# A planned transformer block: a look-ahead on VectorE, the first K and V groups apart, and a new ScalarE cost

## The chip, the cores and the metric

The kernel runs on one core of one Trainium2 chip. The metric is the device time of one launch in microseconds (us). Five engines run in parallel, each through its own queue in order: TensorE (PE, matmuls, with its weight loads shown as PEld), ScalarE (ACT), VectorE (DVE), GpSimd (POOL) and SyncE (SP, which issues the DMAs). They meet through semaphores. A matmul writes PSUM, whose banks hold 512 fp32 values per partition; ACT or DVE then copies or combines the result into SBUF, which is called an evacuation here. Until it is done, the bank can't take another group of matmuls.

## The reference

One block: layer norm, multi-query attention with 32 heads and one shared K and V, a residual, layer norm, a gated feed-forward part, a residual. S = 2048 tokens, D = 1024, head width 32, F = 3584, all in bf16.

```python
q = (x @ wq).reshape(B, S, H, Dh)          # x is the normed input
k = x @ wk                                 # one K and V for all heads
v = x @ wv
scores = einsum("bhqd,bkd->bhqk", q, k) * Dh ** -0.5
o = einsum("bhqk,bkd->bhqd", softmax(scores), v)
h = x0 + o.reshape(B, S, D) @ wo           # x0 is the raw input
g, u = ln(h) @ w_gate, ln(h) @ w_up
out = h + (sigmoid(g) * u) @ w_down
```

## The kernel before

**A plan, then the streams.** The Python program does not emit instructions at once. It first runs a planner (class `Plan`) that keeps its own clock in ns for each engine, and it decides from that clock what each engine does next. Only the resulting order, one list per engine, is then emitted, with semaphore waits between engines. The chip keeps the order; its times are its own. So a changed cost in the plan changes no instruction, only the order of instructions.

- PE is planned by a loop (from line 952). At each step it looks at the plan's PE clock `t`. If the backlog of ACT is under 750 ns and the next scores are possible, it emits a *score visit* (`emit_S`); else it goes on with the current matmul group, or picks a new one from the queues in the order `PRIO`: xT, KV, Q0, OP, GU, D, Q. A group needs a bank of `F_ps` that is free by the plan's clock.
- ACT, DVE, POOL and SP have a heap each. `Plan.step` takes the engine that can start first, at time `s`, and on it the ready operation with the lowest `prio` number (line 89). An operation is ready at `o.ready`, when all that it depends on has ended by the plan. Costs come from `t_act`, `t_dve` and `t_mm`: `occ` is how long the engine is taken, `lat` when the result can be used.

**Priorities on DVE.** 0: the evacuations of attention outputs (L688, L692, L697, L701, L709) and of the up projection (L895). 1: those of the output projection (L777), of Q and K, and the scaling in the first norm (L369). 2: others, also the down projection's (L925). 3: norm statistics and the merge of row sums (L654). 4: the row-sum adds (L647).

**Attention.** Queries are taken in 16 tiles of 128 tokens; each tile has 4 pairs of head groups `G`, and a pair needs 8 visits over the keys. A visit is 8 matmuls (K = 32 rows, four packed in the rows of the array) into `S_ps` (6 banks), and two exponentials (L613) of 128x1024 that ACT writes to probability slots `Pr`. For the softmax sums DVE adds the probability tiles into `Ts` (L647), one add per exponential, merges the halves (L654), and PE multiplies the merged tile by ones. The products with V run in two halves of 8 key tiles, `mk_PV(G, 0)` and `mk_PV(G, 1)`, each 32 matmuls packed in the columns. The first half leaves its bank by one copy to `Oc` (L692); the second by an add to `Oc` (L697) and a transpose of the sums (L709), after which reciprocal, transpose and product follow. A slot comes free once its PV group and its add are done; without two free slots no score visit is possible.

**The rest on PE.** KV, Q, output projection (OP), gate and up (GU) and down (D) are groups of full-size matmuls. All these groups and PV share `F_ps`, which has two banks. GU weights come through a ring of 256 KB pieces by DMA. A gate group leaves its bank by a tanh on ACT (L891), an up group by L895 on DVE. All matmuls are emitted by the helper at L382, so the profile tells them apart by their tiles: `S_ps<-QTb,kT` scores, `F_ps<-Pr,Vb` and `F_ps<-Ts,ones` PV, `F_ps<-ring,hnT` GU, `F_ps<-zone,hact` D, `F_ps<-wo_sb,OT` OP, `F_ps<-zone` KV and Q.

**The start.** `mk_KV(p)` makes K for 256 tokens (8 matmuls with the replicated weight `wk4`) and V for the same tokens (16 small matmuls with `wv_sb`) as one group in one bank. It may be picked when the transposed input, the replicas of wk (4 copies on ACT, L313) and wv are there. K is evacuated to `kT4` (`k_ev`), V to `Vb` (`v_ev`). The first score visit needs K of the first pair and two Q groups, not V. `free_wd` loads pieces of w_down into room that the Q, K and V inputs leave.

Of the kernel before, what the change touches and what calls it, by code (L numbers as in the profile page):

```python
# [14 lines left out]
DH = 32  # L15
LN_EPS_BF16 = 1.0013580322265625e-05
SEM = 75.0


class Op:  # L20
# [16 lines left out]
class Plan:  # L37
# [39 lines left out]
    def step(self, limit):  # L77
        best = None
        for e in self.ENG:
            h = self.heap[e]  # L80
            if h:
                s = max(self.free[e], min(o.ready for o in h))
                if best is None or s < best[0]:
                    best = (s, e)
        if best is None or (limit is not None and best[0] > limit):
            return False
        s, e = best
        h = self.heap[e]
        o = min((o for o in h if o.ready <= s + 1e-9), key=lambda o: (o.prio, o.seq))
        h.remove(o)  # L90
        self.free[e] = s + o.occ
        if o.nbytes:
            go = max(s + 1400.0, self.dma_free["sp"])
            self.dma_free["sp"] = go + o.nbytes / 280.0
            o.end = self.dma_free["sp"] + 900.0
        else:
            o.end = s + o.lat
        o.pos = len(self.lists[e])
        self.lists[e].append(o)
        for u in o.users:  # L100
            u.ready = max(u.ready, o.end)
            u.missing -= 1
            if u.missing == 0:
                self.heap[u.eng].append(u)
        o.users = []
        return True
# [8 lines left out]


def t_act(n):
    return dict(occ=n / 1.2 + 60.0, lat=n / 1.2 + 170.0 + SEM)


def t_dve(n, rate=0.96, fix=158.0):
# [7 lines left out]
def bass_sequential_preLN__grouped_kv_mqa__glu_gated_glu__prompt_kernel(  # L129
# [15 lines left out]
    DT = D // P  # L145
    NT = S // P
# [13 lines left out]
    NPS = 16  # L160
    NX = 4
    NCR = 12
    NB = 3
    NPC = 22
    NST = 3
# [7 lines left out]
    with ExitStack() as es:  # L173
# [12 lines left out]
        kT4 = SB("kT4", [S])  # L186
        Vb = SB("Vb", [NT, DH])
# [22 lines left out]
        F_ps = EC(nc.psum_tensor("F_ps", [P, 2, 512], F32))  # L210
# [92 lines left out]
        wv_ld = dma(lambda: ACT.dma_start(wv_sb, A_wv.rearrange("(a p) j -> p a j", p=P)), "wv", P * DT * DH * 6, [x_ld[1]], prio=0, ring="act")  # L303
# [7 lines left out]
        rep_ops = []  # L311
# [124 lines left out]

        def queue_after_xT(t):
            if t % 2 == 1:
                queues["KV"].append(mk_KV(t // 2))
            if t == 1:  # L440
                for g in range(NG):
                    queues["Q0"].append(mk_Q(g, 0, 256))
            if 1 < t < 8 and t % 2 == 1:
                for g in range(NG):
                    queues["Q"].append(mk_Q(g, (t - 1) * P, 256))
            if t % 4 == 3 and t > 8:
                for g in range(NG):
                    queues["Q"].append(mk_Q(g, (t // 4) * 512, 512))
# [5 lines left out]
        wd_ld = []  # L454
        q_done = collections.Counter()

        def mk_KV(p):
            def atoms(b):
                r = []
                for dt in range(DT):  # L460
                    r.append((mm(F_ps[:, b, 0:256], wk4[:, dt, :], xnT(dt, p * 256, 256), dt == 0, dt == DT - 1),
                              256, rep_ops if dt == 0 else []))
                for k in range(2):
                    for dt in range(DT):
                        r.append((mm(F_ps[:, b, 256 + k * DH:256 + (k + 1) * DH],
                                     xnT(dt, p * 256 + k * P, P), wv_sb[:, dt, :],
                                     dt == 0, dt == DT - 1), DH, [wv_ld] if dt == 0 else []))
                return r

            def after(b, last):  # L470
                fa, fd = both(kT4[:, p * 256:(p + 1) * 256], F_ps[:, b, 0:256])
                k_ev[p] = evac(fa, fd, 256, [last], 1)
                fa, fd = both(Vb[:, 2 * p:2 * p + 2, :],
                              F_ps[:, b, 256:256 + 2 * DH].rearrange("p (a b) -> p a b", a=2))
                v_ev[p] = evac(fa, fd, 64, [last, k_ev[p]], 2)
                free_wd(last)
                return [k_ev[p], v_ev[p]]
            return Group("KV", atoms, lambda: [xT_ev[2 * p], xT_ev[2 * p + 1], rep_ops[-1], wv_ld], after)

        q_ready = collections.defaultdict(dict)  # L480
        q_store = []
# [51 lines left out]

        def free_wd(last):
            for i in list(wd_left):
                if (i < 4 and q_left4[i] == 0 and 2 * i in k_ev and 2 * i + 1 in k_ev) or \
                        (i in (4, 5) and all(q_done[g] == S for g in range(4 * i - 16, 4 * i - 12))) or \
                        (i == 6 and len(k_ev) == NT // 2):
                    wd_left.remove(i)
                    load_wd(4 * i, 4, [last])  # L540

# [404 lines left out]
        v = 0  # L946
        idle = 0

        def known(deps, t):
            return all(d is not None and d.end is not None and d.end <= t for d in deps)  # L950

        while True:
            t = pl.free["pe"]
            pl.advance(t)
            pump(t)
            if v < NV:
                run = max(pl.free["act"], t) + sum(o.occ for o in pl.heap["act"])
                sd = s_ready(v)
                can_s = sd is not None and known(sd, t)
                if can_s and run - t < 750.0:  # L960
                    emit_S(v)
                    v += 1
                    emit_PV(t)
                    idle = 0
                    continue
            else:
                sd, can_s = None, False
            if sd is None and queues["PV"]:
                if emit_PV(t):
                    idle = 0  # L970
                    continue
            if cur is not None:
                fn, n, deps, *cb = cur[1][cur_i]
                if known(deps, t) or not can_s:
                    o = emit_mm(fn, n, deps + (cur[2] if cur_i == 0 else []))
                    o.tag = cur[0].cls
                    if cb and cb[0]:
                        cb[0](o)
                    cur_i += 1
                    if cur_i == len(cur[1]):  # L980
                        bank_rel[cur_b] = cur[0].after(cur_b, o)
# [146 lines left out]
```

The softmax here doesn't subtract the row's maximum and nothing guards it: scores larger than these inputs give would overflow.

## Time and profile before

| what | value |
|---|---|
| time, median of 3 runs | 1103.32 us (1102.48 to 1103.97) |
| span of the profiled run | 1100.7 us |
| exponentials L613 on ACT, 128x1024 | 1024 (1014 into `Pr`, 10 into `wo_sb`), mean length 1078 ns |
| row-sum adds L647 on DVE, 128x1024 bf16 | 864, mean 680 ns for the most frequent form |
| up evacuation L895 on DVE, 128x512 | 112, mean 681 ns |
| `Oc` copy L692, add L697, transpose L709 (most frequent forms) | 60 each, 422, 419 and 441 ns |
| first exponential starts at | 19.76 us |

How to read it: lengths of single instructions overlap on an engine, so the step from one start to the next is shorter than the length. "Idle before" in a line of the profile is time in which the engine did nothing, with the instruction that ended it behind the arrow. Busy time of PE counts modelled ends of matmuls that are pipelined; a PE that reads 98% is not a PE at 98% of its peak.

### The profile page before, as it was taken

The numbers are of one execution on the slowest core, as the hardware profiler recorded it, in microseconds if no ns is written. First come the engines' busy times: TensorE is split into PE (matmuls) and PEld (weight loads), VectorE is DVE, ScalarE is ACT, GpSimd is POOL, SyncE is SP. The second block draws the span as 40 slices with busy tenths as digits, with TensorE's granted clock in tenths as the row PEclk, the third lists the DMA queues.
The fourth block names the chain that finished last, engine by engine and source line by source line (L and its number), as shares of the span: only waits on it lengthen the run. The fifth ranks groups of instructions, "written<-read, shape, count | busy, mean of one in ns | idle before, by whom it ended". The sixth has DMA issues, their size and how long they took to land.

```text
span 1100.7 us, 30884 instructions
## 1 busy us (share of the span) xinstructions
PE 1076.2 (98%) x12635; PEld 473.0 (43%) x12635; DVE 901.1 (82%) x1753; ACT 1009.7 (92%) x1164; POOL 31.1 (3%) x56
## 2 busy tenths in 40 slices
PE   8999999999999999999999999999999999999998
PEld 5663433444344444443444444443444444344443
DVE  8679988898888889898888979897888979898611
ACT  4999999999999999999999999999999999999310
POOL 1100000000000000000000000000000000000000
PEclk9999999999999999999999999999999999999999
DMA  9897499959678595978768594977869595977993
GB/s 260 180 287 231 128 261 243 278 134 277 163 181 233 147 253 131 251 188 214 228 167 237 152 250 127 250 203 199 232 153 245 144 249 149 245 197 170 264 272 118
DMA packets 310988, 228.13 MB, mean 207 GB/s; under 512 B 121920, under 2 KB 302144, under 8 KB 310848
## 3 DMA queue, kind: packets, MB, share of 16 engines
q1 hardware_dynamic: 308768, 226.04, 78.0%
q8 instruction: 99, 1.62, 0.6%
q10 hardware_dynamic: 2080, 0.13, 0.1%
q14 instruction: 41, 0.34, 0.1%
HBM read 195.69 MB, written 7.86 MB: 185 GB/s over the span
## 4 chain that ended last, share of the span: by engine, by line
PE 54%; ACT 24%; DVE 12%; issue 6%; DMA 4%; ACTq 0%; SPq 0%; DVEq 0%
PE F_ps L382 46%; ACT Pr L613 23%; PE S_ps L382 8%; DVE Ts L647 7%; DMA ring<-in_B_w_gate_dram 2%; DMA zone<-in_A_wv_dram 1%; ACT tnh L891 1%; DVE Rc L709 1%; DVE hst L895 1%; DVE Oc L697 1%; DVE h_sb L777 1%; DVE st L321 0%; DVE st L323 0%; DMA ring<-in_B_w_up_dram 0%; DMA zone<-ring 0%
## 5 line engine op out<-in xcount | busy, mean ns | idle before, releaser
L613 ACT ACTIVATE Pr<-S_ps 128x1024 bf16<-128x1024 f32 x1014 | 952.3, 1078 | 6.6 <-PE S_ps L382 6.6
L647 DVE TENSOR_TENSOR Ts<-Ts,Pr 128x1024 bf16<-128x1024 bf16 x732 | 484.2, 680 | 48.2 <-ACT Pr L613 45.2
L382 PE MATMUL F_ps<-ring,hnT 128*128 128x512 bf16 (+1 forms) x1889 | 443.8, 381 | 12.3 <-issue 3.7
L382 PEld LDWEIGHTS F_ps<-ring,hnT 128*128 128x128 bf16 (+1 forms) x1889 | 150.0, 98 | 220.0 <-issue 71.6
L382 PE MATMUL F_ps<-zone,hact 128*32 128x512 bf16 (+1 forms) x1196 | 221.8, 380 | 0.0
L382 PE MATMUL S_ps<-QTb,kT 32*128 32x256 bf16 x4096 | 203.3, 273 | 2.1 <-ACT Pr L613 1.7
L382 PEld LDWEIGHTS S_ps<-QTb,kT 32*128 32x128 bf16 x4096 | 60.6, 92 | 200.4 <-ACT Pr L613 140.6
L382 PE MATMUL F_ps<-Pr,Vb 128*32 128x256 bf16 x4056 | 134.5, 274 | 0.0
L382 PEld LDWEIGHTS F_ps<-zone,hact 128*32 128x32 bf16 (+1 forms) x1196 | 80.0, 97 | 95.9 <-issue 20.6
L891 ACT ACTIVATE tnh<-F_ps 128x512 f32<-128x512 f32 x112 | 73.3, 655 | 52.1 <-PE F_ps L382 52.0
L895 DVE SCALAR_TENSOR_TENSOR hst<-tnh,F_ps 128x512 bf16<-128x512 f32 x112 | 76.3, 681 | 46.0 <-PE F_ps L382 45.9
L382 PEld LDWEIGHTS F_ps<-Pr,Vb 128*32 128x32 bf16 x4056 | 96.9, 96 | 37.4 <-ACT tnh L891 16.1
L647 DVE TENSOR_TENSOR Ts<-Pr 128x1024 bf16<-128x1024 bf16 x126 | 84.7, 683 | 34.0 <-ACT Pr L613 33.9
L382 PE MATMUL F_ps<-zone 128*128 128x256 bf16 (+3 forms) x609 | 75.4, 281 | 5.1 <-DMA zone<-in_A_wv_dram 2.0
L382 PE MATMUL F_ps<-wo_sb,OT 128*128 128x512 bf16 (+1 forms) x271 | 63.7, 381 | 0.1
L382 PEld LDWEIGHTS F_ps<-zone 128*128 128x128 bf16 (+1 forms) x609 | 44.2, 97 | 27.4 <-issue 9.8
L925 DVE SCALAR_TENSOR_TENSOR h_sb<-F_ps,h_sb 128x512 bf16<-128x512 f32 x32 | 22.0, 688 | 40.6 <-PE F_ps L382 40.6
L654 DVE TENSOR_TENSOR Ts<-Ts 128x1024 bf16<-128x1024 bf16 x64 | 44.0, 688 | 1.4
L335 POOL TENSOR_SCALAR zb<-mvb 128x1 bf16<-128x1 bf16 (+1 forms) x24 | 10.9, 455 | 1008.1 <-DVE mvb L331 1008.1
L382 PEld LDWEIGHTS F_ps<-wo_sb,OT 128*128 128x128 bf16 (+1 forms) x271 | 21.4, 97 | 29.5 <-issue 6.8
L714 DVE STREAM_TRANSPOSE Rc<-Ri 128x256 f32<-128x256 f32 x64 | 28.2, 441 | 0.0
L697 DVE TENSOR_TENSOR Oc<-F_ps,Oc 128x256 f32<-128x256 f32 x60 | 25.2, 419 | 2.6 <-PE F_ps L382 2.5
(60 smaller groups left out, 338.4 us busy)
## 6 DMA issues: line engine op xcount, KB each, us to landing
ring<-in_B_w_gate_dram SPq DMA_DIRECT2D x320, 256.0 KB, 4.2
ring<-in_B_w_up_dram SPq DMA_DIRECT2D x320, 256.0 KB, 3.9
zone<-in_B_w_down_dram SPq DMA_DIRECT2D x28, 256.0 KB, 3.9
h_sb<-in_A_x_dram SPq DMA_DIRECT2D x16, 256.0 KB, 5.1
out_dram<-h_sb SPq DMA_DIRECT2D x32, 128.0 KB, 2.9
ring<-in_A_x_dram SPq DMA_DIRECT2D x7, 512.0 KB, 6.4
QTb<-q_scratch SPq DMA_DIRECT2D x14, 256.0 KB, 3.6
q_scratch<-hact SPq DMA_DIRECT2D x16, 128.0 KB, 3.2
```

The costliest lines, as they stand in the source:

```text
L335: f = pl.op("pool", lambda: POOL.tensor_scalar(out=zb[:, ph, sl].unsqueeze(2), in0=mvb[:, ph, sl, 1:2], scalar1=LN_EPS_BF16, scalar2=None, ...
L382: fn = lambda: PE.matmul(o, lhsT=l, rhs=r, start=start, stop=stop, **kw)
L613: exps[u] = pl.op("act", lambda slot=slot, pb=pb: ACT.activation(out=pslot(slot).rearrange("p (a b) -> p a b", a=2), in_=S_ps[:, pb:pb + 2 ...
L647: o = pl.op("dve", lambda T=T, a=a, b=b: DVE.tensor_tensor(out=T, in0=a, in1=b, op=ALU.add), deps, prio=4, **t_dve(1024, 1.92))
L654: merge_ev[G] = pl.op("dve", lambda T4=T4: DVE.tensor_tensor(out=T4[:, :, 0, :], in0=T4[:, :, 0, :], in1=T4[:, :, 1, :], op=ALU.add), [sum ...
L697: a = pl.op("dve", lambda: DVE.tensor_tensor(out=Oc[:, :], in0=O, in1=Ob, op=ALU.add), [last, oc_ev[G], o_ev.get(G - 1)], prio=0, **t_dve( ...
L709: c = pl.op("dve", lambda: DVE.transpose(out=Rc[:, :], in_=R), [last, o_ev.get(G - 1)], prio=0, **t_dve(256))
L714: d = pl.op("dve", lambda: DVE.transpose(out=Rc[:, :], in_=Ri[:, :].unsqueeze(2).to_broadcast([P, 2 * P // DH, DH])), [r], prio=2, **t_dve ...
L777: h_ev[(t, dc)] = pl.op("dve", lambda: DVE.tensor_tensor(out=h_sb[:, t % 4, sl], in0=F_ps[:, b, :], in1=h_sb[:, t % 4, sl], op=ALU.add), [ ...
L891: tanh_of[n] = pl.op("act", lambda: ACT.activation(out=tnh[:, n % 2, :], in_=F_ps[:, b, :], func=ACTF.Tanh, scale=0.5), [last, tn_user.get ...
L895: e = pl.op("dve", lambda: DVE.scalar_tensor_tensor(out=hst[:, n % NST, :], in0=tnh[:, n % 2, :], scalar=1.0, in1=F_ps[:, b, :], op0=ALU.a ...
L925: e = pl.op("dve", lambda: DVE.scalar_tensor_tensor(out=h_sb[:, t % 4, sl], in0=F_ps[:, b, :], scalar=0.5, in1=h_sb[:, t % 4, sl], op0=ALU ...
```

## The change

Three parts, and a fourth that is set to do nothing:

1. In `Plan.step`, if DVE is about to start an operation of priority 3 or more (a row-sum add, a merge, norm statistics), and an operation of priority 0 or 1 will be ready within `AHEAD` = 200 ns, DVE takes that one and waits for it. The purpose is that an evacuation that frees a PSUM bank does not stand behind an add that has just begun.
2. `t_act` gives each ScalarE operation a fixed part of 53 ns instead of 60 in `occ`. Exponentials, tanh and ACT copies are all planned by it. The purpose is to bring the plan's pace to the chip's.
3. For the first 256 tokens K and V are two groups, so that K no longer waits for wv. The frees of `free_wd` ask for V in place of K.
4. `pv_fits` can put off a PV group after a score visit; with `RM` = 0 its first condition always holds.

```diff
+AHEAD = 200.0
+PMAX = 1
...
         o = min((o for o in h if o.ready <= s + 1e-9), key=lambda o: (o.prio, o.seq))
+        if e == "dve" and o.prio >= 3:
+            soon = [x for x in h if x.prio <= PMAX and s < x.ready <= s + AHEAD]
+            if soon:
+                o = min(soon, key=lambda x: x.ready)
+                s = o.ready
         h.remove(o)
...
 def t_act(n):
-    return dict(occ=n / 1.2 + 60.0, lat=n / 1.2 + 170.0 + SEM)
+    return dict(occ=n / 1.2 + 53.0, lat=n / 1.2 + 170.0 + SEM)
...
+    RM = 0
+    PU = 3
...
             if t % 2 == 1:
-                queues["KV"].append(mk_KV(t // 2))
+                for part in (("k", "v") if t == 1 else ("kv",)):
+                    queues["KV"].append(mk_KV(t // 2, part))
...
-            return Group("KV", atoms, lambda: [xT_ev[2 * p], xT_ev[2 * p + 1], rep_ops[-1], wv_ld], after)
+            def first():
+                return [xT_ev[2 * p], xT_ev[2 * p + 1]] + ([rep_ops[-1]] if "k" in part else []) + ([wv_ld] if "v" in part else [])
+            return Group("KV", atoms, first, after)
...
-                if (i < 4 and q_left4[i] == 0 and 2 * i in k_ev and 2 * i + 1 in k_ev) or \
+                if (i < 4 and q_left4[i] == 0 and 2 * i in v_ev and 2 * i + 1 in v_ev) or \
...
+        def pv_fits():
+            left = 8 if cur is None else len(cur[1]) - cur_i
+            return left >= RM or len(queues["PV"]) > 1 or len(p_free) < PU or v >= NV
...
                     emit_S(v)
                     v += 1
-                    emit_PV(t)
+                    if pv_fits():
+                        emit_PV(t)
```

More of the change, by code (lines that the diff above doesn't have):

```diff
@@ L455, in bass_sequential_preLN__grouped_kv_mqa__glu_gated_glu__prompt_kernel, with mk_KV @@
         q_done = collections.Counter()
-        def mk_KV(p):
+        def mk_KV(p, part):
             def atoms(b):
                 r = []
-                for dt in range(DT):
+                for dt in range(DT if "k" in part else 0):
                     r.append((mm(F_ps[:, b, 0:256], wk4[:, dt, :], xnT(dt, p * 256, 256), dt == 0, dt == DT - 1),
                               256, rep_ops if dt == 0 else []))
-                for k in range(2):
+                for k in range(2 if "v" in part else 0):
                     for dt in range(DT):
@@ L470, in after @@
             def after(b, last):
[L471 to L477, printed above, removed]
-            return Group("KV", atoms, lambda: [xT_ev[2 * p], xT_ev[2 * p + 1], rep_ops[-1], wv_ld], after)
+                rel = []
+                if "k" in part:
+                    fa, fd = both(kT4[:, p * 256:(p + 1) * 256], F_ps[:, b, 0:256])
+                    k_ev[p] = evac(fa, fd, 256, [last], 1)
+                    rel.append(k_ev[p])
+                if "v" in part:
+                    fa, fd = both(Vb[:, 2 * p:2 * p + 2, :],
+                                  F_ps[:, b, 256:256 + 2 * DH].rearrange("p (a b) -> p a b", a=2))
+                    v_ev[p] = evac(fa, fd, 64, [last, k_ev[p]], 2)
+                    rel.append(v_ev[p])
+                    free_wd(last)
+                return rel
+            def first():
+                return [xT_ev[2 * p], xT_ev[2 * p + 1]] + ([rep_ops[-1]] if "k" in part else []) + ([wv_ld] if "v" in part else [])
+            return Group("KV", atoms, first, after)
         q_ready = collections.defaultdict(dict)
@@ L535, in free_wd @@
             for i in list(wd_left):
-                if (i < 4 and q_left4[i] == 0 and 2 * i in k_ev and 2 * i + 1 in k_ev) or \
+                if (i < 4 and q_left4[i] == 0 and 2 * i in v_ev and 2 * i + 1 in v_ev) or \
                         (i in (4, 5) and all(q_done[g] == S for g in range(4 * i - 16, 4 * i - 12))) or \
-                        (i == 6 and len(k_ev) == NT // 2):
+                        (i == 6 and len(v_ev) == NT // 2):
                     wd_left.remove(i)
```

## The prediction

> **What bounds the kernel now.** I read the page first (busy shares, then the 40 slices), then the windows by stage, then the waits, and last the timeline around single waits.
>
> ```profile
> PE 1076.2 (98%) x12635; PEld 473.0 (43%) x12635; DVE 901.1 (82%) x1753; ACT 1009.7 (92%) x1164; POOL 31.1 (3%) x56
> PE   8999999999999999999999999999999999999998
> ACT  4999999999999999999999999999999999999310
> ```
>
> Two engines are full at once. ACT is full until its exponentials end near 1026 us. PE is full to the end, and after 1026 us it is alone, with gate, up and down matmuls left over. So the end is set by the sum of PE's work and PE's waits; ACT and DVE count only through the waits they cause on PE. The windows show where PE still has slack:
>
> ```profile
> 0.00:60.00 60.00, 53.53 (x722) 36.77 (x726) 43.52 (x124) 41.44 (x62) 8.57 (x24) 1.00 0.96 230
> 60.00:300.00 240.00, 228.86 (x2916) 101.55 (x2912) 211.78 (x405) 236.76 (x268) 3.89 (x6) 1.00 0.84 222
> 300.00:1025.00 725.00, 721.06 (x8551) 300.79 (x8539) 626.27 (x1190) 723.98 (x826) 17.88 (x24) 1.00 0.76 199
> 1025.00:1100.70 75.70, 72.77 (x474) 33.89 (x466) 19.56 (x36) 7.56 (x12) 0.79 (x2) 1.00 0.80 217
> ```
>
> (Columns: stretch, length, then busy us of PE, PEld, DVE, ACT, POOL, clock, DMA share, GB/s.) PE is idle 6.5 us in the first 60, 11.1 in the next 240, 3.9 in the long middle, 2.9 in the tail. From about 315 us the timeline repeats every 124.63 us, which is two query tiles (128 exponentials, 14 tanh).
>
> ```profile
> 439.30:563.90 124.60, 124.10 (x1476) 51.86 (x1475) 107.69 (x204) 124.60 (x143) 3.02 (x4) 1.00 0.75 202
> PEld F_ps L382 <- DVE Rc L709: 12.7, 26, 1.0
> PE F_ps L382 <- DMA zone<-in_A_wv_dram: 2.0, 1, 2.0
> ```
>
> Here DVE is busy 107.69 of 124.60 us, 86%, so it has room to wait. The two wait lines (us in total, times, longest) name the buffers in question: PE's weight load stands before a group whose PSUM bank the transpose at L709 still reads, and at the start PE stands 2.0 us for wv. Now one such bank wait from the timeline:
>
> ```profile
> 250.40 0.28 PE L382 MATMUL F_ps<-Ts,ones 128*32 128x256 bf16 x4
> 250.70 0.69 DVE L647 TENSOR_TENSOR Ts<-Ts,Pr 128x1024 bf16<-128x1024 bf16 x1 [0.22 <-ACT Pr L613]
> 251.31 0.42 DVE L697 TENSOR_TENSOR Oc<-F_ps,Oc 128x256 f32<-128x256 f32 x1
> 251.65 0.44 DVE L709 STREAM_TRANSPOSE Rc<-F_ps 128x256 f32<-128x256 f32 x1
> 252.14 0.60 PE L382 MATMUL F_ps<-ring,hnT 128*128 128x512 bf16 x2 [0.70 <-DVE Rc L709]
> ```
>
> The PV group ends at 250.68. Evacuations that were not held up start 0.05 us after such an end, so L697 could start at 250.73. A row-sum add started at 250.70, three hundredths before, and kept DVE for 0.61 us. The evacuation ran late by 0.58, and PE idled 0.70. That is exactly the pattern the change is made for.
>
> **What the Trainium skill says.** Perfetto Trace Analysis, Identifying the Most-Contended Engine, warns that matmul busy time is no measure of distance to the roofline. The trace agrees: the matmul columns of one period come to 106.7 us at 2.4 columns per ns (GU 224 and D 112 and OP 32 matmuls of 512 columns, 78.5 us, and scores and PV packed by four, 28.2), while PE reads 124.10 busy. The rest is changes between row, column and full mode, which this change leaves in number as they are (one score visit per two exponentials). PSUM — Partial Sum Buffer, Engine vs sequencer instructions, says the ScalarE, VectorE and GpSimd queues are strict FIFO; the lines above agree, since L697 does not pass the add. Perfetto Trace Analysis, Optimizing Scalar/DVE Operations, gives about 51 ns of overhead for a Scalar instruction on PSUM. The trace agrees: undisturbed exponentials start 904 ns apart (1024/1.2 is 853.3, so 51 is left), tanh to exponential 0.48 us (501.57 to 502.05). The plan before has 60, the new one 53.
>
> **The change, part by part.**
>
> *The hold.* It removes no instruction; it changes DVE's order. For every DVE evacuation of priority 0 or 1 I compared, in the timeline, the start of the instruction before it with the end of the matmul group that it empties. Of 264 such evacuations 75 stand behind an add that started less than 200 ns before they were ready. Together these 75 start 35.0 us late; holding the adds would cost DVE 9.7 us of idling (130 ns each), about 1 us per period, which 86% busy can carry. What waits behind a held add: the next adds, the merge (L654), and through it the second-half PV group and its probability slots. The adds already wait 79.1 us in total for exponentials, so a push of 0.2 us plus one evacuation (0.34 to 0.60 us) mostly lands in slack. But most of the 35 us never reaches PE, since PE uses the other bank meanwhile. What reaches it: between 60 and 300 us I find seven waits of 0.45 to 1.13 us behind a DVE evacuation (140.05, 158.11, 205.31, 230.68, 252.14, 271.09, 284.27; sum 5.3 us), each with an add that started within 60 ns of the ready time. The 0.55 us or so of add in six or seven of them is 3.4 us, an upper value. In the repeating part five waits per period at L709 make 1.23 us, but there the add started 430 to 505 ns early and is outside the 200 ns, so the hold does not touch them. The hold: 0 to 3.4 us; I take 2.3, because the plan's clock and the chip's differ by more than 60 ns at places and some waits will come up elsewhere.
>
> *The recalibration.* It takes 7 ns from each ScalarE entry of the plan. In plan time a period of ACT goes from 128 x 913.3 + 14 x 486.7 = 123.7 us to 128 x 906.3 + 14 x 479.7 = 122.7. The chip's ACT can do it in 128 x 904 + 14 x 478 = 122.4, with semaphore waits (many steps are 920 instead of 904, mean about 908) in 123.1. PE without its five bank waits needs 124.63 - 1.23 - about 0.3 of others = 123.1. So a plan that asks for scores a little sooner takes slack from both: the period can fall from 124.63 to 123.1 at best, and to about 123.8 if half the waits stay. Over (1025 - 315)/124.63 = 5.7 periods that is 4.7 us, with 0 and 8.7 as bounds. What earlier scores take from matmul filler goes to the tail at the same cost on PE, so only removed waits count. In the tail DMA is busy 0.80 and PE waits for it only 0.3 us, so a few us more there are carried.
>
> *The first K and V groups.* K (8 matmuls of 256 columns, 40.0/320 = 0.125 us each, 1.0 us) no longer waits for wv. The copies of wk end at 12.99 + 1.33 = 14.32, so K runs inside the 2.0 us in which PE stood, and V (16 x 4.6/128 = 0.6 us) waits for wv until 17.18 as before. 1.0 us of PE work moves into idle time; the first score goes from 19.31 to 17.8 or 18.4. I take 0.8 of it as kept at the end.
>
> *The rest.* `pv_fits` with RM = 0 is always true, since `left` is never below 0: nothing. The frees for w_down now ask for v_ev instead of k_ev, which is set in the same place for all groups but the first: nothing. In the preamble the hold can also put off a bn_stats by up to 0.2 us for a scaling; the scaling comes first by as much: nothing.
>
> Sum: 2.3 + 4.7 + 0.8 = 7.8. I take 1 off for the reshuffled plan, whose waits nobody chose: 6.8 us, 1103.3 - 6.8 = 1096.5 us.
>
> **The rivals.** *All bank waits go.* 5.3 in front, 5.7 x 1.23 = 7.0 in the middle, 2.0 for wv: 1103.3 - 14.3 = 1089.0. For it: every one of these waits is on an evacuation or on wv. Against: five per period are out of the hold's reach.
> *Hidden anyway.* DVE's late evacuations matter only where PE has no second bank, and the middle stays paced by PE; only K's 1.0 us comes through: 1102.3. For it: PE idles just 3.9 us in 725. Against: the 124.63 contains 1.5 us of waits that the modelled matmul ends partly hide.
> *Slower: ACT and PE locked tighter.* With 906 in the plan against about 908 on the chip, ACT has no reserve, PE meets busy score banks, and DVE waits in order for evacuations while adds and merges pile up behind. If the new repeating pattern has ten bank waits per period instead of five: 5.7 x 1.23 = 7.0 more, less 1.0 and 1.0 of the start and front: 1108.3. For it: the pattern repeats to a hundredth of a us, so one bad coincidence is paid 5.7 times or more. Against: in the middle PE waits for ACT at no score now, and the new figure is nearer to the measured 904.
>
> **How the numbers follow.** Likeliest case 0.52, all waits gone 0.16, hidden 0.16, slower 0.16. Faster by over 0.2% means below 1101.1: the first two, 0.68. Within it: the hidden case, 0.16. Slower: 0.16. The range 1089.5 to 1105.5 leaves out half of the all-gone case (0.08) and most of the slower one (0.12).
>
> **What would show it.** Hold: waits on L709 and L692 between 60 and 300 us down from some 5 us to under 3; DVE evacuations that stand behind a just started add rare; DVE's own waits "<-PE F_ps" up by some 10 us, busy time unchanged. Recalibration: a repeating period near 123.8 us, exponentials ending near 1020 us and a tail of 73 to 78 us. K and V: first exponential near 18.5 instead of 19.76. Wrong would be: a period of 124.6 or more, new PE waits for ACT at S_ps, or PE waits for ring loads in the tail.

## The result, and the profile after

| | before, measured again beside it | after |
|---|---|---|
| time, median (lowest to highest), us | 1103.64 (1102.48 to 1106.69) | 1095.7 (1094.77 to 1096.45) |
| ratio, 95% interval | | 0.9923 (0.9901 to 0.9946) |
| span of the profiled run, us | 1100.7 | 1092.9 |

The changed kernel is 7.9 us faster, 0.8%; 6.8 us was forecast. The sizes inside the sum, however, lay elsewhere. Line numbers have moved: L382 is now L391 (matmuls), L613 L631 (exponentials), L647 L665 (row-sum adds), L692 L710 and L697 L715 (`Oc`), L709 L727 (transpose), L895 L913 (up evacuation).

The page of the kernel after, busy shares and two of the 40-slice rows:

```profile
PE 1076.1 (98%) x12775; PEld 480.5 (44%) x12775; DVE 903.4 (83%) x1755; ACT 1006.5 (92%) x1162; POOL 22.9 (2%) x56
PE   8999999999999999999999999999999999999998
ACT  4899999999999999999999999999999999999510
```

The windows of after by stage (stretch, length, busy us of PE, PEld, DVE, ACT, POOL, clock, DMA share, GB/s):

```profile
0.00:60.00 60.00, 54.39 (x727) 36.08 (x731) 43.75 (x125) 41.36 (x60) 8.75 (x24) 1.00 0.93 234
60.00:300.00 240.00, 237.66 (x3001) 107.66 (x2994) 215.88 (x419) 237.31 (x269) 4.68 (x8) 1.00 0.83 222
300.00:1025.00 725.00, 719.38 (x8693) 307.35 (x8692) 628.10 (x1184) 722.50 (x826) 8.65 (x22) 1.00 0.80 203
1025.00:1092.90 67.90, 64.68 (x366) 29.38 (x363) 15.62 (x29) 5.37 (x9) 0.79 (x2) 1.00 0.78 205
```

PE is busy 1076.1 us as before (1076.2). Summed over the trace, its idle time falls from 24.5 to 16.8 us, by 7.7, and the span by 7.8. More than all of that goes between 60 and 300 us, where PE was busy 228.86 of 240 and is now busy 237.66; between 300 and 1025 us its idle time grows, from 3.9 to 5.6. Part of the new busy time is not work: when the plan finds nothing for PE, the kernel puts in a matmul of 256 columns into a spare bank (`F_ps<-kT,ident`), 8 of them before and 32 after, 29 of these between 60 and 300 us. From start to start they take 1.2 us before and 3.9 after.

That the busy time is equal nevertheless has a second reason. PE works in three modes here, full (`128*128` in the lines), row (`32*128`, the scores) and column (`128*32`, PV), and the number of changes of mode has fallen: counted from the weight loads in order, there are 1094 before and 1061 after. If a PV group follows a score visit at once, instead of after some full matmuls, one change is saved. By the starts in the trace, PE goes from scores to PV in 0.197 us and from scores to a full matmul in 0.200, but from a full matmul to PV in 0.31, where the next full matmul would start after 0.216. So a saved change is worth about 0.1 us (an estimate from these steps), and 33 of them 3 us.

Where the gain shows depends on where one looks. By the starts of the same exponentials:

| kernel | first | 320th | last (1024th) | span | between 320th and last | after the last began |
|---|---|---|---|---|---|---|
| before | 19.76 | 340.17 | 1026.15 | 1100.7 | 685.98 | 74.5 |
| after | 19.02 | 338.04 | 1022.69 | 1092.9 | 684.65 | 70.2 |

The 7.8 us are 2.1 up to the 320th exponential, 1.3 in the repeating stretch and 4.3 in the tail. The tail is shorter because PE did more gate, up and down matmuls in the front, in time that it spent idle before: after the last exponential began, 325 matmuls of 512 columns are left in the kernel before and 303 in the changed one.

All waits of PE between 60 and 300 us that the profile lists, first of before, then of after (total us, times, longest):

```profile
PE F_ps L382 <- DMA ring<-in_B_w_up_dram: 2.9, 3, 1.2
PE F_ps L382 <- issue: 2.5, 4, 1.1
PE F_ps L382 <- DMA ring<-in_B_w_gate_dram: 1.6, 2, 0.9
PE F_ps L382 <- DVE Rc L709: 1.4, 2, 0.7
PE S_ps L382 <- ACT Pr L613: 1.3, 3, 0.9
PE F_ps L382 <- DVE Rc L701: 1.0, 2, 0.7
```

```profile
PE S_ps L391 <- ACT wo_sb L631: 0.8, 1, 0.8
PE F_ps L391 <- issue: 0.5, 1, 0.5
PE F_ps L391 <- DVE Rc L727: 0.4, 1, 0.4
PE F_ps L391 <- DMA ring<-in_B_w_up_dram: 0.3, 1, 0.3
```

The waits that end at "issue" all end 0.10 us after a DVE evacuation, so they belong to the bank waits. These fall from 4.9 us to 0.9. But the waits for weights from the ring fall as much, from 4.5 us to 0.3. The hold isn't aimed at them, and no run here separates what removed them: the order of the loads changed with that of everything else.

Over the whole timeline the DVE evacuations behind an add that began less than 200 ns before they were ready fall from 75 (35.0 us late in all) to 37 (15.5).

One bank wait stays in the repeating part, once per tile. The timeline of after:

```profile
570.52 1.06 PE L391 MATMUL F_ps<-Pr,Vb 128*32 128x256 bf16 x32
571.41 0.69 DVE L665 TENSOR_TENSOR Ts<-Ts,Pr 128x1024 bf16<-128x1024 bf16 x1 [0.71 <-ACT Pr L631]
572.02 0.42 DVE L710 COPY Oc<-F_ps 128x256 f32<-128x256 f32 x1
572.54 0.81 PE L391 MATMUL F_ps<-ring,hnT 128*128 128x512 bf16 x3 [0.31 <-issue]
```

The PV group ends at 571.58, so the copy could start at 571.63. The add began 0.22 us before that. This looks like a case just outside the look-ahead of 200 ns, but the hold goes by the plan's clock, and there the same add begins 0.51 us before its evacuation is ready. The copy starts 0.39 late, and PE idles 0.31 by this line. So a look-ahead in plan time removes coincidences of the plan; some of those on the chip it doesn't see.

### The profile page after: what moved, and what is told of

Read it like the earlier page. It is cut to its first block, busy times and chain, and to the rows that moved or that the text cites. A ratio compares the mean times of both kernels' runs of the same rounds, so it can differ in the third digit from the quotient of the medians.

```text
span 1092.9 us, 31226 instructions
## 1 busy us (share of the span) xinstructions
PE 1076.1 (98%) x12775; PEld 480.5 (44%) x12775; DVE 903.4 (83%) x1755; ACT 1006.5 (92%) x1162; POOL 22.9 (2%) x56
## 4 chain that ended last, share of the span: by engine, by line
PE 89%; ACT 4%; DMA 4%; DVE 1%; issue 1%; ACTq 0%; SPq 0%; DVEq 0%
PE F_ps L391 75%; PE S_ps L391 14%; ACT Pr L631 4%; DMA ring<-in_B_w_up_dram 1%; DMA zone<-in_A_wv_dram 1%; DVE Ts L665 1%; ACT wo_sb L631 1%; DMA zone<-ring 0%; DMA ring<-in_B_w_gate_dram 0%; DMA hnT<-hn 0%; DMA ring<-in_A_x_dram 0%; DVE Rc L727 0%; DVE hst L913 0%; ACT hact L282 0%; ACT tnh L909 0%
## 5 line engine op out<-in xcount | busy, mean ns | idle before, releaser
L631 ACT ACTIVATE Pr<-S_ps 128x1024 bf16<-128x1024 f32 x1014 | 961.1, 1174 | 6.8 <-PE S_ps L391 6.5
L665 DVE TENSOR_TENSOR Ts<-Ts,Pr 128x1024 bf16<-128x1024 bf16 x732 | 480.4, 677 | 46.0 <-ACT Pr L631 44.3
L391 PE MATMUL F_ps<-ring,hnT 128*128 128x512 bf16 (+1 forms) x2045 | 433.2, 380 | 6.6 <-issue 4.3
L391 PEld LDWEIGHTS F_ps<-ring,hnT 128*128 128x128 bf16 (+1 forms) x2045 | 155.8, 97 | 202.3 <-issue 55.7
L391 PE MATMUL F_ps<-zone,hact 128*128 128x512 bf16 (+1 forms) x1145 | 226.0, 380 | 0.0
L391 PE MATMUL S_ps<-QTb,kT 32*128 32x256 bf16 x4096 | 203.3, 273 | 1.3 <-ACT wo_sb L631 0.8
L391 PEld LDWEIGHTS S_ps<-QTb,kT 32*128 32x128 bf16 x4096 | 60.6, 92 | 205.8 <-ACT Pr L631 161.1
L391 PE MATMUL F_ps<-Pr,Vb 128*32 128x256 bf16 x4056 | 134.5, 274 | 0.0
L665 DVE TENSOR_TENSOR Ts<-Pr 128x1024 bf16<-128x1024 bf16 x126 | 85.9, 683 | 56.5 <-ACT Pr L631 56.4
L909 ACT ACTIVATE tnh<-F_ps 128x512 f32<-128x512 f32 x112 | 83.3, 744 | 47.6 <-PE F_ps L391 47.6
L391 PEld LDWEIGHTS F_ps<-zone,hact 128*128 128x128 bf16 (+1 forms) x1145 | 80.7, 97 | 97.6 <-issue 25.1
L391 PEld LDWEIGHTS F_ps<-Pr,Vb 128*32 128x32 bf16 x4056 | 96.8, 96 | 32.2 <-issue 18.6
L913 DVE SCALAR_TENSOR_TENSOR hst<-tnh,F_ps 128x512 bf16<-128x512 f32 x112 | 76.3, 681 | 27.3 <-PE F_ps L391 27.1
L391 PE MATMUL F_ps<-zone 128*128 128x256 bf16 (+4 forms) x612 | 75.9, 280 | 3.3 <-DMA zone<-in_A_wv_dram 1.2
L391 PE MATMUL F_ps<-wo_sb,OT 128*128 128x512 bf16 (+1 forms) x277 | 64.0, 381 | 0.4 <-DVE Rc L727 0.4
L391 PEld LDWEIGHTS F_ps<-zone 128*128 128x128 bf16 (+1 forms) x612 | 43.8, 97 | 27.1 <-issue 8.7
L943 DVE SCALAR_TENSOR_TENSOR h_sb<-F_ps,h_sb 128x512 bf16<-128x512 f32 x32 | 21.9, 684 | 25.0 <-PE F_ps L391 25.0
L391 PEld LDWEIGHTS F_ps<-wo_sb,OT 128*128 128x128 bf16 (+1 forms) x277 | 21.5, 97 | 29.2 <-issue 7.1
L710 DVE COPY Oc<-F_ps 128x256 f32<-128x256 f32 x60 | 25.3, 422 | 5.1 <-PE F_ps L391 3.2
L715 DVE TENSOR_TENSOR Oc<-F_ps,Oc 128x256 f32<-128x256 f32 x60 | 25.3, 422 | 3.6 <-PE F_ps L391 2.4
```

The costliest lines, as they stand in the source:

```text
L391: fn = lambda: PE.matmul(o, lhsT=l, rhs=r, start=start, stop=stop, **kw)
L631: exps[u] = pl.op("act", lambda slot=slot, pb=pb: ACT.activation(out=pslot(slot).rearrange("p (a b) -> p a b", a=2), in_=S_ps[:, pb:pb + 2 ...
L665: o = pl.op("dve", lambda T=T, a=a, b=b: DVE.tensor_tensor(out=T, in0=a, in1=b, op=ALU.add), deps, prio=4, **t_dve(1024, 1.92))
L710: oc_ev[G] = pl.op("dve", lambda: DVE.tensor_copy(out=Oc[:, :], in_=O), [last, o_ev.get(G - 1)], prio=0, **t_dve(256))
L715: a = pl.op("dve", lambda: DVE.tensor_tensor(out=Oc[:, :], in0=O, in1=Ob, op=ALU.add), [last, oc_ev[G], o_ev.get(G - 1)], prio=0, **t_dve( ...
L909: tanh_of[n] = pl.op("act", lambda: ACT.activation(out=tnh[:, n % 2, :], in_=F_ps[:, b, :], func=ACTF.Tanh, scale=0.5), [last, tn_user.get ...
```

## The experiments

Theory A: the hold carries the gain, by bank waits that PE no longer meets. Theory B: the new ScalarE cost carries it, by a shorter repeating period. Theory C: the plan is an order that falls into one repeating pattern or another, and any small edit redraws it.

All but the changed kernel were timed in five rounds beside the kernel before (its median 1104.91 for the a runs, 1105.13 for b, 1105.63 for c). "Per tile" is the mean time of a query tile over the last 11 tiles; "front" is PE's idle time between 60 and 300 us; "tail" is the time from the last exponential's start. In the c runs 159 to 174 matmuls are missing from each trace, which makes PE look idle where it isn't, so their front is not given.

Differences of a few us need one caution. PE's granted clock, as a mean over a run, was between 0.991 and 1.0 of full speed. The kernel before took 1103.93 us (median) in its 20 runs at 1.0 of the c rounds, 1106.20 in 29 runs at 0.998 and 1108.08 in 9 runs at 0.997. Since 39 of those 59 runs were below 1.0 and only 3 of c1's 22, the ratios of c1, c4 and others come out somewhat low. The column "at 1.0" therefore has the median of the runs at 1.0 alone, with their number.

| run | hold | cost | K and V | median us | ratio (95%) | at 1.0 (runs) | per tile | front | tail |
|---|---|---|---|---|---|---|---|---|---|
| before | no | 60 | together | | 1 | 1103.69 (11), 1103.77 (18), 1103.93 (20) | 62.36 | 11.1 | 74.5 |
| after | 200 | 53 | apart | 1095.7 | 0.9923 (0.9901 to 0.9946) | 1095.70 (4) | 62.24 | 2.3 | 70.2 |
| a1 | 200 | 60 | together | 1101.78 | 0.9975 (0.9965 to 0.9985) | 1100.24 (6) | 62.56 | 1.8 | 72.2 |
| a2 | no | 53 | together | 1112.59 | 1.0077 (1.0062 to 1.0091) |  | 62.74 | 7.9 | 79.7 |
| a3 | no | 60 | apart | 1108.29 | 1.0035 (1.0019 to 1.0052) | 1107.89 (6) | 62.47 | 8.7 | 82.9 |
| a4 | no | 53 | apart | 1111.95 | 1.0067 (1.0055 to 1.0080) | 1110.72 (1) | 62.77 | 7.8 | 80.8 |
| b1 | 200 | 53 | together | 1098.20 | 0.9923 (0.9896 to 0.9950) | 1096.45 (3) | 62.25 | 3.1 | 70.2 |
| b2 | 200 | 60 | apart | 1103.72 | 0.9984 (0.9972 to 0.9995) | 1103.66 (3) | 62.24 | 6.2 | 78.2 |
| b3 | 400 | 53 | apart | 1103.71 | 0.9980 (0.9967 to 0.9992) | 1102.59 (18) | 62.61 | 3.2 | 72.3 |
| b4 | 60 | 53 | apart | 1115.60 | 1.0086 (1.0057 to 1.0115) |  | 63.33 | 8.0 | 79.1 |
| c1 | undone in DVE's list | 53 | apart | 1103.96 | 0.9984 (0.9974 to 0.9993) | 1103.60 (19) | 62.76 | | 70.2 |
| c2 | only in DVE's list | 60 | together | 1105.66 | 0.9998 (0.9989 to 1.0008) | 1104.20 (5) | 62.34 | | 74.5 |
| c3 | 200 | 56 | apart | 1109.19 | 1.0033 (1.0016 to 1.0051) | 1106.46 (7) | 63.59 | | 69.9 |
| c4 | 200 | 50 | apart | 1101.29 | 0.9954 (0.9938 to 0.9969) | 1101.29 (6) | 62.35 | | 72.8 |

What a repeating stretch of two tiles consists of can be read from the starts of PE's matmuls. "Steps" is their sum if each takes the usual step of its kind, "waits" what they take beyond it (c1's from the steps of the changed kernel, whose PE order it has):

| run | changes of mode | steps, us | waits, us | two tiles, us |
|---|---|---|---|---|
| before | 138 | 122.7 | 1.9 | 124.63 |
| after, b1 | 132 | 122.1 | 2.1 | 124.19 |
| a1 | 138 | 122.7 | 2.3 | 125.03 |
| a2 | 135 | 122.4 | 2.9 | 125.35 |
| a3 | 136 | 122.5 | 2.2 | 124.69 |
| b2 | 128 | 121.7 | 2.5 | 124.19 |
| c1 | 132 | 122.1 | 3.1 | 125.24 |

So the shorter period of the changed kernel comes from six changes of mode fewer, not from shorter waits. Against c1, the same PE order without the hold, the waits are 1 us shorter.

**a1, the hold alone.** The changed kernel with the other two parts undone.

```diff
-    return dict(occ=n / 1.2 + 53.0, lat=n / 1.2 + 170.0 + SEM)
+    return dict(occ=n / 1.2 + 60.0, lat=n / 1.2 + 170.0 + SEM)
...
-                for part in (("k", "v") if t == 1 else ("kv",)):
+                for part in ("kv",):
```

> Hold alone: ScalarE cost back at 60, K and V in one group. Theory H (the hold removes PE's waits for DVE between 60 and 300 us): PE idle there falls from 11.1 us to under 5, the time falls by 5 us or more to 1095-1099. Theory R (the new pace does it, the hold is idle order): PE idle stays near 11 us there and the time is 1101-1104. Theory N (any reshuffle of the plan moves the waits about by chance): some value between 1096 and 1110 without fewer evacuations behind a just started add.

Measured: 0.9975. The front window reads

```profile
60.00:300.00 240.00, 238.19 (x2977) 105.83 (x2966) 214.50 (x415) 237.34 (x268) 5.01 (x8) 1.00 0.82 225
```

PE's front idle is as low as in the full change, with the old cost. But the tiles then settle at 62.52 us instead of 62.32, with as many changes of mode as before and longer waits, which gives part of it back.

**a2, the new cost alone.** Against the kernel before:

```diff
-    return dict(occ=n / 1.2 + 60.0, lat=n / 1.2 + 170.0 + SEM)
+    return dict(occ=n / 1.2 + 53.0, lat=n / 1.2 + 170.0 + SEM)
```

> ScalarE cost 53 alone, no hold, K and V in one group. Theory R: the repeating period falls from 124.63 us for two tiles to 124.2 or less and the time by 4 us or more, to 1099 or less. Theory H: the period changes by under 0.5 us, PE idle between 60 and 300 us stays near 11 us, time 1100-1104. Theory N: anything between 1096 and 1110, with no relation to the period.

Measured: slower by 0.77%. The tiles alternate between 62.42 and 62.93 us, where the kernel before has 62.29 and 62.34. A smaller cost in the plan has not shortened the period. Theory B falls as a theory of this part alone.

**a3, K and V apart alone.** The edits of `mk_KV` and `free_wd`, without the hold and with cost 60.

> First K and V groups apart, alone. From the sums of the prediction: first exponential about 1 to 1.5 us earlier than 19.76 us, PE wait for wv 2.0 us down to about 1.2, time 1102.5 (0.8 less). Theory N: the early shift moves all later groups, so that the time differs by several us either way.

Measured: slower by 0.35%. The last exponential begins 2.8 us earlier than before (1023.32), yet the tail is 82.9 us. An earlier start doesn't survive a plan that leaves more for the tail: 348 matmuls of 512 columns are left there, 325 before. Why the plan leaves more was not followed.

**a4, all but the hold.**

```diff
-AHEAD = 200.0
+AHEAD = 0.0
...
-        if e == "dve" and o.prio >= 3:
+        if AHEAD > 0 and e == "dve" and o.prio >= 3:
```

> The whole change without the hold. Theory H: most of the 7.9 us is lost, 1100-1103, and PE waits for DVE evacuations between 60 and 300 us are back at 4 us or more. Theory R: time stays at 1095-1098. Parts that add up would give this one the sum of the gains of the new cost alone and of K and V alone.

Measured: slower by 0.67%, with the same 62.42 and 62.93 pattern as a2:

```profile
60.00:300.00 240.00, 232.16 (x2943) 103.11 (x2933) 211.33 (x407) 237.94 (x270) 3.92 (x6) 1.00 0.81 222
```

PE is idle 7.8 us here, against 2.3 in the changed kernel. The change needs the hold; without it the two other parts lose. The three ratios of the single parts multiply to 0.9975 x 1.0077 x 1.0035 = 1.0087, while the whole is 0.9923. The parts can't be added.

**b1, all but K and V apart.**

```diff
-                for part in (("k", "v") if t == 1 else ("kv",)):
+                for part in ("kv",):
```

> Hold and new ScalarE cost, K and V in one group. Theory I (the hold turns the new cost from a loss into a gain, K and V matter little): period near 62.1 us per tile as in the whole change, time 1095-1099. Theory A (K and V are needed for it): 1101 or more.

Measured: 0.9923, like the full change; the interval is some 3 us to each side, too wide to tell 1 us. The profiled runs differ as the split would have it: the first exponential begins at 20.37 instead of 19.02, the last at 1024.19 instead of 1022.69, the tail is the same, and the span is 1.5 us longer.

**b2, all but the new cost.** `t_act` with 60 again.

> Hold and K and V apart, ScalarE cost 60. Theory I: as with the hold alone, period 62.3 to 62.5 us per tile, time 1099-1103. If parts added up, it would be hold alone (0.9975) times K and V alone (1.0035), 1104.

Measured: 0.9984. This run is the test of theory B under the hold. Both it and the changed kernel repeat every 62.10 us, so the short period comes without the new cost. From the 320th exponential to the last b2 takes 1025.61 - 340.95 = 684.66 us, against 684.65; that these agree so closely is chance, since either stretch has odd tiles in it (63.72 in b2, where the clock fell to 0.83 between 340 and 350 us; 62.80, 62.38 and 62.82 in the changed kernel). What b2 loses is the front (2.9 us later at the 320th exponential, with one wait of 2.85 us for a ring load at 154.08 and a clock of 0.83 between 150 and 160) and the tail (78.2 against 70.2). Among its groups by line, within the part of the trace after 1000 us:

```profile
L391 PE MATMUL F_ps<-kT,ident 128*128 128x256 bf16 x36 | 4.3, 272 | 0.0
```

These 36 fill-in matmuls stand at 1079 and 1085 us: the plan found no work for PE there. PE also waits 2.2 us for DMAs in this tail. The changed kernel has no fill-in after 300 us. The cost of 53 gave a plan without that hole, not a faster pace.

**b3 and b4, the look-ahead at 400 and at 60.**

```diff
-AHEAD = 200.0
+AHEAD = 400.0
```

> The whole change with a look-ahead of 400 ns. In the trace of the changed kernel the one bank wait left per tile (0.48 us) stands behind an add that started 0.22 us before its evacuation was ready, just outside 200. Theory H: that wait goes, 11 tiles x 0.48 us = 5 us less, 1090-1092. Theory D (DVE has no more room: longer holds push adds and merges into the PV groups): 1097 or more, with more PE waits behind merges.

> The whole change with a look-ahead of 60 ns. The waits that the prediction named in the front had adds starting within 60 ns of the ready time. If these are the ones that matter, the front keeps its gain (PE idle 2-4 us between 60 and 300 us) and the time is 1096-1100. If the hold works by the many evacuations between 60 and 200 ns, the front is back at 8 us or more idle and the time near that without the hold, 1110.

Measured: 0.9980 and 1.0086. At 60 the front is idle 8.0 us, as without a hold; at 400 it is 3.2, but the tiles become irregular, from 62.0 to 63.1 us. Both expectations took the trace's times for the plan's. The wait that the first counts on was out of reach of 400 too, since its add starts 508 ns ahead by the plan's clock. And the adds of the seven front waits start 19 to 115 ns ahead by that clock, four of them more than 60. Lengths near 200 weren't tried.

**c1, the held evacuations put back.** Every plan comparison so far compares two different orders on PE. Here the plan is that of the changed kernel, and so are the lists of PE, ACT, POOL and SP. Afterwards each of the 91 additions, merges and statistics that were held goes back ahead of the evacuation that had passed it, in DVE's list alone.

```diff
+                first = o
                 o = min(soon, key=lambda x: x.ready)
+                o.over = first
...
+        for o in list(lists["dve"]):
+            if o.over is not None and id(o.over) not in seen:
+                seen.add(id(o.over))
+                lists["dve"].remove(o.over)
+                lists["dve"].insert(lists["dve"].index(o), o.over)
```

> The plan of the whole change, made with the hold; afterwards each of the 91 held operations is put back in front of the evacuation that it was held for, in DVE's queue alone. The orders of PE, ACT, GpSimd and the DMAs are those of the changed kernel, instruction by instruction. Theory H1 (the hold works by what DVE does on the chip): evacuations run late again, PE waits, 1105 or more. Theory H2 (the hold works because the plan, with banks free earlier, gives PE another order, and the chip would keep most of it anyway): 1096-1100.

Measured: 0.9984, and 0.9923 with the held order; the intervals don't touch. At a clock of 1.0 it is 1103.60 us, as slow as the kernel before. One place of the two timelines, the same matmuls in both (some lines between are left out). First the changed kernel:

```profile
219.24 0.28 PE L391 MATMUL F_ps<-Ts,ones 128*32 128x256 bf16 x4
219.58 0.42 DVE L715 TENSOR_TENSOR Oc<-F_ps,Oc 128x256 f32<-128x256 f32 x1
219.89 0.40 PE L391 MATMUL S_ps<-QTb,kT 32*128 32x256 bf16 x8
219.92 0.44 DVE L727 STREAM_TRANSPOSE Rc<-F_ps 128x256 f32<-128x256 f32 x1
220.22 1.05 PE L391 MATMUL F_ps<-ring,hnT 128*128 128x512 bf16 x4
220.28 0.65 DVE L665 TENSOR_TENSOR Ts<-Ts,Pr 128x1024 bf16<-128x1024 bf16 x1
```

Then c1, whose lines are numbered three higher:

```profile
220.99 0.28 PE L394 MATMUL F_ps<-Ts,ones 128*32 128x256 bf16 x4
221.42 0.69 DVE L668 TENSOR_TENSOR Ts<-Ts,Pr 128x1024 bf16<-128x1024 bf16 x1 [0.22 <-ACT Pr L634]
221.64 0.40 PE L394 MATMUL S_ps<-QTb,kT 32*128 32x256 bf16 x8
221.96 0.10 PEld L394 LDWEIGHTS F_ps<-ring,hnT 128*128 128x128 bf16 x1 [0.21 <-issue]
222.03 0.42 DVE L718 TENSOR_TENSOR Oc<-F_ps,Oc 128x256 f32<-128x256 f32 x1
222.37 0.44 DVE L730 STREAM_TRANSPOSE Rc<-F_ps 128x256 f32<-128x256 f32 x1
222.91 0.38 PE L394 MATMUL F_ps<-ring,hnT 128*128 128x512 bf16 x1 [0.87 <-issue]
```

In the changed kernel PV ends at 219.52, the add to `Oc` starts 0.06 later, and the transpose ends at 220.36. PE meanwhile has a score visit and, at 220.22, the last matmul of an up group; its next group starts at 220.46, 0.10 after the transpose and hardly later than it could. In c1 PV ends at 221.27. The row-sum add stands first in DVE's queue and is itself short of an exponential, so DVE idles until 221.42; then the add takes its 0.61 us. The transpose ends at 222.81, and PE goes on 0.10 later. The profile names no releaser there ("issue"); the transpose is read from the times. Of the 0.87 idle a part is false: the weight load at 221.96 has no matmul in this trace, where the changed kernel has that last matmul 4 ns after the load. With its length of 0.39 put in, PE idles 0.55. The same group is in every repeating tile of c1, for instance with 0.98 us at 380.45, of which 0.66 is left in the same way.

By the exponentials c1 runs like this: first 18.80, 320th 342.02, last 1032.43, span 1102.6. Against the changed kernel that is 4.0 us in the front, 5.8 in the repeating stretch (62.62 us per tile against 62.10) and nothing in the tail. The order on DVE alone, on these PE and ACT orders, is worth 1103.96 - 0.9923 x 1105.63 = 6.8 us by the ratios, and 1103.60 - 1095.70 = 7.9 us between the runs at a clock of 1.0: the whole gain.

**c2, the held order on the plan of before.** The reverse: plan and other lists of the kernel before, and in DVE's list alone 75 evacuations moved ahead of 62 operations that the plan starts less than 200 ns before the evacuation is ready.

```diff
+            if o.prio <= 1:
+                i = lists["dve"].index(o)
+                while i and lists["dve"][i - 1].prio >= 3 and o.ready - 200.0 <= lists["dve"][i - 1].start < o.ready:
+                    i -= 1
+                lists["dve"].remove(o)
+                lists["dve"].insert(i, o)
```

> The plan of the kernel before, unchanged; afterwards, in DVE's queue alone, each evacuation of priority 0 or 1 that became ready within 200 ns after the start of a priority 3 or 4 operation is put in front of it. All other orders are those of the kernel before. Theory H1: the seven front waits of the prediction go, 3 to 4 us less, 1100-1102. Theory H2: PE's order was made for the late banks and does not use the early ones, so under 1 us, 1103-1105.

Measured: 0.9998, no change. The tail is 74.5 us as before and the repeating stretch 685.7 (before 686.0). Yet the bank waits of the front did get shorter. One of them, first before, then c2:

```profile
140.05 0.59 PE L382 MATMUL F_ps<-ring,hnT 128*128 128x512 bf16 x2 [1.06 <-issue]
140.58 0.40 PE L382 MATMUL S_ps<-QTb,kT 32*128 32x256 bf16 x8
```

```profile
141.46 0.38 PE L383 MATMUL F_ps<-ring,hnT 128*128 128x512 bf16 x1 [0.60 <-issue]
142.24 0.40 PE L383 MATMUL S_ps<-QTb,kT 32*128 32x256 bf16 x8 [0.40 <-ACT Pr L614]
```

PE idles 0.60 or less (a matmul's record is missing just before) instead of 1.06 for the bank, and then waits 0.40 for an exponential at the next score visit. Between 60 and 300 us its waits for exponentials grow from 3 (1.3 us) to 10 (3.8 us). The order brings the next score visit soon after the bank, and gives PE nothing else to do until ACT is ready for it. In these places an earlier bank would be worth something only if PE's order had other work there.

**c3 and c4, the cost at 56 and at 50, with the hold.**

```diff
-    return dict(occ=n / 1.2 + 53.0, lat=n / 1.2 + 170.0 + SEM)
+    return dict(occ=n / 1.2 + 56.0, lat=n / 1.2 + 170.0 + SEM)
```

> The whole change with a ScalarE cost of 56 instead of 53. Theory P (pace: the nearer to the measured 904 ns, the better, evenly between 60 and 53): 1098-1101, between the two measured with the hold. Theory L (the middle locks into one of a few repeating patterns, and which one is not told by the cost): any of 62.0 to 62.7 us per tile, 1095-1108, not in order of the cost.

> The whole change with a ScalarE cost of 50 instead of 53, 3 ns under what the chip takes in undisturbed steps where 53 is 2 ns over. Theory P: within 2 us of the whole change, 1095-1099, with a little more waiting of PE for score banks. Theory L: anywhere in 1095-1108.

Measured, with b2 and the change in the row: cost 60 gives 0.9984, 56 gives 1.0033, 53 gives 0.9923, 50 gives 0.9954. There is no order in it, and none between the runs at a clock of 1.0 (1103.66, 1106.46, 1095.70, 1101.29 us). At 56 the tiles take 62.3 to 65.6 us and never settle; the longest three hold stretches at a clock of 0.83 to 0.94, the others don't. (A cost of 50 puts the plan's step at 903.3 ns, 0.7 under the measured 904, not the 3 that the expectation says.) A pace that fits the chip would have given a curve with its best near the measured step; theory C fits these four.

## Why the prediction came out as it did

*What bounds.* Right. PE was called the bound to the end and its waits the only thing to win. Its busy time stayed, its idle time fell by 7.7 us, the span by 7.8. Not foreseen: 24 more fill-in matmuls, 2.7 us, count as busy. And the sentence that the changes of mode stay "in number as they are" failed: 33 of them went, some 3 us, all in the repeating part. That the two cancel in the busy time is luck.

*The hold, 2.3 us with 0 to 3.4 as bounds.* The mechanism was right, the size too small. The pair of timelines above is the queueing that the prediction described, with the add itself kept waiting as a second form of it, and c1 prices it at 6.8 to 7.9 us on the plan of the change. The term that failed is "the hold does not touch them" for the repeating part: it was argued from the five waits of the old pattern. In the new order on PE there is a wait of 0.66 us per tile that the hold does remove, 0.52 us of the tile's time net, and 5.8 us of c1's profiled loss lies there. The other omission: I counted only waits that PE already had. The planner sees the bank come free earlier and gives PE another order, and c2 shows that on the old order the earlier bank is worth nothing. Two of the seven front waits were also misread. At 140.05 the add did not start just before the ready time but 0.21 after it, having waited for an exponential at the head of the queue. At 284.27 the profile names a load into the ring, which landed 0.05 before PE went on, while DVE's add to `Oc` had ended 0.17 before. And the front gained 4.2 us from waits for such loads, which the prediction counted nowhere.

*The recalibration, 4.7 us.* Wrong, in cause and in size. (A slip in its sum: with a mean step of 908 ns ACT's period is 122.9 us, not 123.1.) The period fell from 124.63 to 124.2 us, not to 123.8, and the repeating stretch gave 1.3 us. Even that isn't the cost's: b2 repeats in the same 62.10 us per tile with the old cost, and a2, with the new cost alone, has a longer period. The step that failed is "a plan that asks for scores a little sooner takes slack from both". ACT's pace in the plan, a percent more or less, isn't what sets the period; PE's own steps do, with the number of changes of mode and the waits that the order happens to have (122.1 and 2.1 us after, 122.7 and 1.9 before). In the changed plan 53 did help (0.9923 against 0.9984), by a front without a long wait and a tail without holes, and 56 and 50 did not do as well.

*K and V, 0.8 us.* Supported, not settled. PE's wait for wv falls from 2.0 to 1.2 us. In the profiled runs the first exponential starts at 18.2 to 19.8 us in the kernels with K apart (median 18.8) and at 19.75 to 21.9 in those without (median 20.2; the 21.9 is c2, whose clock was 0.89 to 0.94 between 10 and 30 us), so the start does gain about a microsecond. Between b1 and the change 1.5 us of span remain at the end, but the timed runs can't tell that much. Alone, the same edit came out slower through its tail.

*The rest, nothing,* and *the reshuffle, 1 us lost.* The changed kernel holds no sign against the first. The second was the right worry at the wrong size: the reshuffle swings by 10 us and more between neighbouring plans (c3 to the change: 1.0033 against 0.9923, 12 us).

So the total of 6.8 came near 7.9 because a hold that was too small and a recalibration that was too large cancelled. Of the signs named in advance, these came: the bank waits in the front, the rarer evacuations behind an add. These didn't: the first exponential began at 19.02 instead of 18.5, the tail is 70.2 us where 73 to 78 was forecast, the last exponential began at 1022.7 instead of 1020, and DVE's waits for PE at `F_ps` fell from 105.2 to 74.7 us instead of rising by 10, while its waits for exponentials rose from 79.1 us to 100.6:

```profile
DVE Ts L665 <- ACT Pr L631: 100.6, 225, 1.2
```

Of the rivals, "slower" is what a2, a4 and c3 did, by longer patterns as it said, though not the changed kernel. What the patterns of 62.10, 62.32, 62.52 and 62.67 us per tile consist of, the table of steps and waits says. Open is why a plan falls into one of them, and so how much of the gain another small edit would lose. None of the runs was faster than the change; b1 equals it.

## What to carry to other kernels

When a planner writes the order of all queues, an edit of one rule changes every queue, and comparing two plans doesn't tell what the rule is worth. Reorder one queue's list alone, with the others kept, in both directions (c1, c2): it separates the rule's own worth from the luck of the plan. Before a recalibrated constant is believed, run its neighbours; if 60, 56, 53 and 50 give no curve, the constant picks a plan, it doesn't fit a model. And price a removed wait not by the waits in the old trace alone, but by what the bound engine can be given to do once the buffer comes earlier. Where the bound engine looks equally busy in two versions, take its busy time apart (fill-in, changes of mode, work) before the idle time is taken for the whole gain.

## What the runs showed of the hardware

The Trainium skill, PSUM — Partial Sum Buffer, Engine vs sequencer instructions, says that the queues of ScalarE, VectorE and GpSimd are strict FIFO. c1 shows a cost of it that I had only half seen: the blocking instruction needn't be running. At 378.96 in c1 DVE stood idle for 0.23 us behind an add that waited for an exponential, nearly all of it with a ready evacuation next in line (PV had ended at 378.70), and with the add itself PE lost 0.66 us to it.

A change of mode on PE has a price: over the runs in the table, the sum of PE's steps in two tiles falls from 122.7 to 121.7 us while the changes fall from 138 (before, a1) to 128 (b2), 0.1 us each. The profile counts that time as busy.

The repeating patterns are exact: the changed kernel, b1 and b2 have typical tiles of 62.10 us each, and c1's loss comes back at the same place in each tile. One coincidence in an order is paid 11 times over.
